# The list of pieces in another order, and GpSimd's subtractions in operations of 512 elements

## The chip, the cores and the metric

The kernel runs on one core of a Trainium2 chip. Its engines work side by side, each through its own instructions in program order: TensorE (PE, with its weight loads as PEld), VectorE (DVE), ScalarE (ACT), GpSimd (POOL) and SyncE (SP), which here issues nearly all transfers. The metric is the time of one execution on the device in microseconds, as the median of several runs.

## The reference

Attention over 32 pooled memory rows per head, and then a two-layer network whose nonlinearity is h - tanh(h):

```python
a = phi - np.max(phi, axis=2, keepdims=True)
a = np.exp(a)
a = a / (np.sum(a, axis=2, keepdims=True) + 1e-09)
k_m = np.einsum('bhsm,bhsd->bhmd', a, k)
v_m = np.einsum('bhsm,bhsd->bhmd', a, v)
scores = scale * np.matmul(q, k_m.transpose(0, 1, 3, 2))
scores = scores - np.max(scores, axis=-1, keepdims=True)
attn = np.exp(scores)
attn = attn / (np.sum(attn, axis=-1, keepdims=True) + 1e-09)
attn_out = np.matmul(attn, v_m)
...
x = attn_out.transpose(0, 2, 1, 3).reshape(B * S, H * D)
h = x @ w_in
g = h - np.tanh(h)
out = g @ w_out
```

There are 8 batches with 8 heads, 576 positions, head width 64 and 32 memory rows; x is 4608 x 512, `w_in` 512 x 2048 and `w_out` 2048 x 512. The weights come as 64-bit floats.

## The kernel before

**Arithmetic.** The pooled values are multiplied into `w_in` first (the pieces P, with result `pp` in PSUM, `ph` and `pl` in SBUF), so that h is a product of the attention weights (256 per token: 8 heads with 32 rows) with P. Every operand of a product is split into a high half in float16 and a low half, the rest after subtracting the high one, and three products of halves stand for one of full precision. ScalarE casts the high half; the low half is a subtraction. The nonlinearity is a polynomial in h times h cubed.

**Tiling.** The 4608 tokens are 18 units (u) of 256, the 2048 features four blocks (fb) of 512. For each unit and block there are: `H` (`mm1`, L598), the product h into the PSUM tile `hs`, and its square on ScalarE (L616); `a` (`cubic`, L621), VectorE (L630), ScalarE (L632) and VectorE again (L642); `g` (L659), the high half; `c` (`a_low`, L664), the low half on GpSimd, or `cv` on VectorE; and `M` (`mm2`), the product with `w_out`. From unit 4 on, `M` uses seven products of half-size blocks instead of eight (L749). For these `f` (`s_forms`, L668) makes four sums of blocks on VectorE (L675), and `s` (`s_high`, L679) their halves, the high ones on ScalarE (L682), the low ones on GpSimd (L684). `BS`, `BF`, `BH` and `BL` make the same sums of `w_out` once. `E` (`evict`, L795) puts the results of a unit together (L800 to L811) and stores them.

**Attention.** For each batch: `FX`, `FA`, `KA`, `KB`, `KR`, `Q`, `QT` load; `X`, `YX`, `XU`, `XT` (batches 0 and 1) or `XP`, `YM`, `YE` make the exponentials, where `YM` calls `less_top` (L208) on GpSimd; `V`, `N`, `U`, `UV` pool and normalise; `S`, `AM`, `AE`, `AD`, `AT`, `AS` are scores and softmax; `P` and `PL` (L578) make P and its low half. `P` takes the one buffer of the PSUM pool `ps_a`, which `S`, `V`, `U`, `XP` and `NI` use too. `T` converts two blocks of a weight from 64-bit words, `L`, `Lv` and `Lp` make their low halves on GpSimd, VectorE or TensorE. `i0:gg` loads block 0 of `w_in` into a buffer named gg, `i6:kv3` blocks 6 and 7 into kv3, `o2` block 2 of `w_out`; `k5:q` loads a block again for a check, which `CW` reads. `Z` (`warm`, L846) is a pair of products whose result is not used.

**Order.** The string `ORDER` (L71 to L130) is the program: its words are taken one after another, each emits one piece, and a word that stands again emits the next step of the same piece (`T0 T0 T0 T0` is three steps on VectorE and the cast on ScalarE). Each engine works through its instructions in that order (`in_order`, L915), SyncE's loads too, and waits only for what an instruction reads or the buffer it writes. There is a second way through the kernel for inputs outside a range (`wide_path`), which doesn't run here.

Of the kernel before, what the change touches and what calls it, by code (L numbers as in the profile page):

```python
# [75 lines left out]
XU1 a0.0 XT1 XU1 T11 T11 a0.0 KA1 o1:gg T11 V1.0 Lv10 g0.0 V1.1 N1 H1.1 H1.0 a1.0 a1.0 o0:pp2 T8 T8 c0.0 U1 UV1 o10:pp5 KA2 UV1 U1 S1.0 T8 H1.1 S1.0  # L76
AM1.0 T8 Lv8 T11 L11 L11 k1:q a1.0 g1.0 FA2 CW1 ap1.1 ap1.1 H0.1 H0.1 i10:kv3 S1.1 S1.1 AM1.1 ap1.1 ap0.1 AM1.0 AE1.0 AD1.0 c1.0 AM1.1 AE1.1 T5 M0.0
M0.0 AD1.0 AD1.1 g1.1 P1.0 P1.0 cv1.1 W0 PL1.0 M1.0 M1.0 ap0.1 AT1.0 AS1.0 AD1.1 AT1.1 ASv1.1 AS1.0 ap0.1 i8:kv2 T4 T5 T5 M1.1 T4 g0.1 cv0.1 FX2 P1.1
P1.1 o8:gg ASv1.1 T5 M1.1 OP1 L5 H2.0 H2.0 o9:pp4 PL1.1 i14:kv3 L5 X2 OP1 a2.0 M0.1 OP0 M0.1 T4 OP0 T12 T12 H2.1 a2.0 a2.0 T12 T4 Lv4 H2.1 a2.1 g2.0
XP2 Y2 a2.1 H3.0 H3.0 M2.0 T12 a2.1 g2.1 o11:gg T13 c2.0 M2.0 H3.1 H3.1 Lv12 ap3.0 ap3.0 P0.2 P0.2 T13 T13 YE2 T13 ap3.0 g3.0 c2.1 M2.1 M2.1 PL0.2  # L80
i12:kv2 V2.0 L13 T7 T7 a3.1 a3.1 KB2 V2.1 N2 T6 T7 T6 T6 H0.2 cv3.0 OP2 OP2 Q2.1 T7 P1.2 H0.2 Q2.0 a3.1 Lv7 FA3 M3.0 M3.0 P1.2 T6 Lv6 g3.1 H1.2 H1.2
PL1.2 a0.2 BS0 a0.2 P0.3 a0.2 P0.3 PL0.3 L13 c3.1 M3.1 M3.1 g0.2 c0.2 ap1.2 ap1.2 U2 U2 o12:kv2 T14 ap1.2 o14:kv3 OP3 OP3 H1.3 T15 W1 UV2 T15 UV2 M0.2
T15 H1.3 a1.3 S2.0 FQ3 S2.0 AM2.0 g1.2 c1.2 H0.3 T15 a1.3 a1.3 g1.3 c1.3 P1.3 P1.3 T14 H2.2 PL1.3 Lv15 H0.3 S2.1 H2.2 a0.3 a2.2 M0.2 a0.3 a2.2 S2.1
AM2.0 AE2.0 a0.3 H2.3 T14 AM2.1 AM2.1 X3 P2.0 P2.0 T14 Lv14 g0.3 H2.3 c0.3 AE2.1 ADv2.1 M1.2 M1.2 M1.3 M1.3 AD2.0 AD2.0 a2.3 a2.2 a2.3 a2.3 g2.2 c2.2
R1 O1 H3.2 H3.2 PL2.0 O1 AT2.0 P2.1 AS2.0 AS2.0 ADv2.1 AT2.1 ASv2.1 P2.1 M0.3 M0.3 ap3.2 ap3.2 H4.0 BF0 g2.3 c2.3 PL2.1 BH0 ap3.2 H4.0 R0 O0 O0 BL0
P2.2 a4.0 P2.2 PL2.2 g3.2 a4.0 BS1 H4.1 QT3.0 P2.3 a4.0 BF1 H3.3 P2.3 f4.0 BH1 PL2.3 cv3.2 M2.2 M2.2 H3.3 H4.1 ASv2.1 g4.0 c4.0 ap3.3 ap3.3 XP3 M2.3
M2.3 Y3 XX BL1 ap3.3 g3.3 a4.1 H4.2 s4.0 s4.0 R2 O2 O2 M3.2 cv3.3 H4.2 a4.2 a4.1 a4.1 f4.1 a4.2 a4.2 f4.2 H4.3 H4.3 g4.1 c4.1 BS2 R3 M3.2 M3.3 M3.3
s4.1 YE3 KR3.0 O3 KR3.1 V3.0 M4.0 M4.0 M4.0 M4.0 a4.3 a4.3 O3 BF2 BH2 g4.2 s4.1 V3.1 M4.1 a4.3 f4.3 QT3.1 BL2 N3 U3 H5.0 UV3 UV3 U3 S3.0 c4.2 BS3 S3.0
AM3.0 s4.2 M4.1 M4.1 M4.1 H5.0 a5.0 s4.2 M4.2 P3.0 BF3 M4.2 a5.0 H5.1 P3.0 a5.0 M4.2 M4.2 f5.0 AM3.0 g4.3 c4.3 k2:q BH3 s4.3 PL3.0 H5.1 a5.1 AE3.0
AD3.0 P3.1 s4.3 s5.0 H5.2 P3.1 PL3.1 BL3 M4.3 a5.1 a5.1 S3.1 S3.1 M4.3 M4.3 M4.3 H5.2 s5.0 W3 AM3.1 g5.0 c5.0 E4 f5.1 M4.3 g5.1 s5.1 AD3.0 P3.2 E4  # L90
a5.2 a5.2 M5.0 E4 E4 E4 H5.3 H5.3 M5.0 AT3.0 c5.1 E4 s5.1 M5.1 k0:e AS3.0 AS3.0 a5.2 g5.2 f5.2 a5.3 CW0 AM3.1 a5.3 FQ4 a5.3 M5.0 AE3.1 c5.2 M5.1 AD3.1
s5.2 H6.0 H6.0 P3.2 k4:q a6.0 a6.0 AD3.1 PL3.2 s5.2 M5.0 M5.1 M5.1 g5.3 a6.0 H6.1 H6.1 f5.3 W2 f6.0 M5.2 M5.2 M5.2 M5.2 s5.3 s5.3 a6.1 g6.0 P3.3 P3.3
H6.2 a6.1 c5.3 c6.0 s6.0 X4 XP4 H6.2 PL3.3 a6.1 CW2 AT3.1 AS3.1 FA4 s6.0 YM4 a6.2 a6.2 KR4.0 f6.1 a6.2 M5.3 M5.3 M5.3 E5 M5.3 M5.3 CW4 H6.3 s6.1 s6.1
E5 M6.0 KR4.1 g6.1 H6.3 a6.3 a6.3 M6.0 E5 AS3.1 H7.0 c6.1 M6.1 E5 E5 E5 YM4 M6.1 M6.0 YE4 V4.0 f6.2 M6.0 M6.1 g6.2 a6.3 f6.3 M6.1 H7.0 a7.0 s6.2 a7.0
s6.3 a7.0 f7.0 H7.1 H7.1 a7.1 g6.3 s6.2 a7.1 V4.1 N4 c6.2 k3:e M6.2 M6.2 g7.0 M6.2 M6.2 a7.1 f7.1 QT4.0 c6.3 SI0 s7.0 s6.3 U4 UV4 H7.2 U4 SS0 H7.2
a7.2 s7.0 M6.3 M6.3 M6.3 E6 M6.3 CW3 FQ5 M6.3 c7.0 E6 S4.0 UV4 a7.2 H7.3 a7.2 f7.2 g7.2 E6 E6 s7.1 s7.1 M7.0 g7.1 S4.0 H7.3 c7.2 k5:e NI0 M7.0 M7.0
M7.0 QT4.1 S4.1 NI0 E6 E6 AM4.0 a7.3 a7.3 H8.0 a7.3 f7.3 g7.3 X5 H8.0 S4.1 c7.1 M7.1 M7.1 M7.1 s7.2 s7.2 a8.0 H8.1 M7.2 M7.2 M7.2 a8.0 a8.0 s7.3 AM4.0
AE4.0 s7.3 c7.3 AM4.1 M7.1 M7.2 H8.1 AD4.0 AD4.0 a8.1 M7.3 M7.3 a8.1 a8.1 f8.0 f8.1 g8.0 M7.3 g8.1 E7 E7 AT4.0 s8.0 AM4.1 s8.0 P4.0 P4.0 PL4.0 H8.2
H8.2 a8.2 AE4.1 AD4.1 E7 E7 a8.2 a8.2 M7.3 M7.3 E7 f8.2 P4.1 P4.1 E7 H8.3 H8.3 a8.3 FA5 CW5 c8.0 M8.0 M8.0 M8.0 M8.0 c8.1 AS4.0 AS4.0 H9.0 s8.1 s8.1
KR5.0 M8.1 g8.2 c8.2 a8.3 a8.3 PL4.1 XP5 M8.1 M8.1 s8.2 M8.1 H9.0 KR5.1 g8.3 a9.0 H9.1 a9.0 f8.3 s8.3 a9.0 f9.0 YM5 H9.1 s8.2 P4.2 P4.2 PL4.2 YM5 M8.2  # L100
M8.2 QT5.0 M8.2 YE5 M8.2 c8.3 V5.0 g9.0 AD4.1 a9.1 a9.1 a9.1 g9.1 f9.1 s8.3 H9.2 H9.2 s9.0 M8.3 M8.3 M8.3 AT4.1 k6:e V5.1 M8.3 M8.3 E8 E8 c9.0 s9.0 N5
E8 SI1 a9.2 E8 E8 s9.1 P4.3 P4.3 PL4.3 c9.1 E8 a9.2 M9.0 a9.2 f9.2 M9.0 g9.2 M9.0 U5 SS1 U5 UV5 FQ6 s9.2 UV5 H9.3 s9.1 M9.1 NI1 H9.3 NI1 a9.3 AS4.1
M9.0 CW6 S5.0 S5.0 QT5.1 s9.2 a9.3 M9.1 a9.3 f9.3 AS4.1 H10.0 AM5.0 M9.1 g9.3 M9.1 k7:q H10.0 a10.0 AM5.0 AE5.0 AD5.0 CW7 S5.1 c9.2 S5.1 a10.0 H10.1
a10.0 f10.0 M9.2 H10.1 a10.1 s9.3 c9.3 P5.0 M9.2 M9.2 M9.2 P5.0 PL5.0 AM5.1 a10.1 a10.1 X6 s9.3 s10.0 s10.0 H10.2 H10.2 a10.2 AD5.0 M9.3 W5 M9.3 f10.1
a10.2 a10.2 g10.0 c10.0 M9.3 M9.3 AT5.0 s10.1 M9.3 XP6 YM6 H10.3 P5.1 H10.3 M10.0 E9 E9 M10.0 E9 M10.0 k8:e CW8 P5.1 AM5.1 AE5.1 s10.1 E9 E9 E9 M10.0
AS5.0 g10.2 AS5.0 g10.1 W4 c10.1 a10.3 H11.0 FA6 f10.2 s10.2 M10.1 M10.1 a10.3 a10.3 P5.2 KR6.0 M10.1 M10.1 H11.0 PL5.1 a11.0 a11.0 a11.0 P5.2 PL5.2
H11.1 c10.2 YM6 YE6 g10.3 V6.0 s10.2 M10.2 M10.2 M10.2 H11.1 QT6.0 KR6.1 M10.2 f10.3 s10.3 s10.3 f11.0 s11.0 a11.1 a11.1 AD5.1 AD5.1 AT5.1 H11.2 AS5.1
# [284 lines left out]
def split_path(ctx, tc, c, ins, out):  # L392
# [271 lines left out]
    def a_low(u, fb, eng):  # L664
        for x, (hi, lo) in a_parts(u, fb):
            eng.tensor_tensor(lo, x, hi, op=ALU.subtract)  # L666
# [463 lines left out]
```

## Time and profile before

| | |
|---|---|
| three runs, us | 671.54, 672.4, 670.91 |
| median, us | 671.54 |
| the profiled execution: its own time, us | 672.69 |
| its span from first to last instruction, us | 670.9 |
| mean granted TensorE clock | 0.984 |
| ScalarE busy, us | 402.4 |
| moved by DMA | 85.03 MB, mean 127 GB/s |

The span is 1.8 us shorter than the time of the execution it was taken from. In the profile an engine's busy time is the sum of its instructions' spans without overlap. Rows of a group give the line, engine, operation, tiles out<-in, sizes and count, then total busy us and mean ns, then the engine's idle time just before these instructions and what ended it. Rows of the timeline give start and duration in us. "x2" in a row of the timeline merges two instructions that follow each other. The granted clock is 1.00 at full speed.

### The profile page before, as it was taken

How to read it: one execution, taken by the hardware profiler on the slowest of the kernel's cores; microseconds unless marked ns; L12 is line 12 of the kernel's file. 1: busy time of each engine (PE TensorE's matmuls, PEld its weight loads, DVE VectorE, ACT ScalarE, POOL GpSimd, SP SyncE). 2: the span in 40 equal slices, each digit the busy share in tenths (PEclk: the TensorE clock that was granted, in tenths of full speed). 3: DMA queues.
4: the chain of work that ended last, by engine and by line, in shares of the span. 5: the costliest groups of instructions: out<-in, count | busy, mean ns of one | idle time of the engine just before them, and what ended most of it. 6: DMA issues, size and time to landing. Idle time of an engine off the chain costs nothing. (4 is left out here: it accounts for less than half of the span.)

```text
span 670.9 us, 16165 instructions
## 1 busy us (share of the span) xinstructions
PE 633.5 (94%) x6882; PEld 485.1 (72%) x6882; DVE 584.8 (87%) x818; ACT 402.4 (60%) x541; POOL 371.5 (55%) x257
## 2 busy tenths in 40 slices
...
GB/s 330 310 355 216 195 190 205 149 97 64 34 198 107 67 34 68 146 169 127 2 69 114 163 99 37 150 94 130 36 147 164 162 75 88 30 127 69 122 95 38
DMA packets 25872, 85.03 MB, mean 127 GB/s; under 512 B 2752, under 2 KB 2752, under 8 KB 25024
## 3 DMA queue, kind: packets, MB, share of 16 engines
...
## 5 line engine op out<-in xcount | busy, mean ns | idle before, releaser
L666 POOL TENSOR_TENSOR g<-h,g 128x256 f16<-128x256 f32 (+1 forms) x123 | 149.0, 1232 | 111.0 <-ACT g L662 106.6
L609 PEld LDWEIGHTS <-ph 128*128 128x128 f16 x2304 | 177.5, 98 | 28.0 <-issue 12.0
L684 POOL TENSOR_TENSOR f<-s,f 128x1024 f16<-128x1024 f32 x56 | 125.7, 2245 | 84.1 <-ACT f L682 65.6
L609 PE MATMUL hs<-ah,ph 128*128 128x256 f16 (+3 forms) x1152 | 151.5, 246 | 2.1 <-DVE h L630 2.0
L761 PEld LDWEIGHTS <-f 128*128 128x128 f16 x1344 | 128.8, 98 | 31.4 <-issue 12.1
L761 PE MATMUL x<-bt,f 128*128 128x256 f16 x1008 | 128.4, 273 | 4.4 <-DVE r L802 2.0
L609 PE MATMUL hs<-al,ph 128*128 128x256 f16 (+3 forms) x576 | 127.6, 246 | 0.2 <-POOL al L551 0.2
L632 ACT ACTIVATE u<-u,beta 128x1024 f32<-128x1024 f32 x72 | 82.6, 1147 | 61.7 <-DVE h L630 60.7
L642 DVE SCALAR_TENSOR_TENSOR h<-u,h 128x1024 f32<-128x1024 f32 x72 | 98.5, 1369 | 19.8 <-ACT u L632 19.5
L761 PEld LDWEIGHTS <-g 128*128 128x128 f16 x1008 | 98.6, 98 | 13.7 <-issue 1.1
L616 ACT ACTIVATE u<-hs 128x1024 f32<-128x1024 f32 x54 | 55.1, 1020 | 52.9 <-PE hs L609 31.2
L662 ACT ACTIVATE g<-h 128x512 f16<-128x512 f32 (+2 forms) x128 | 68.4, 580 | 23.6 <-DVE h L642 19.7
L630 DVE SCALAR_TENSOR_TENSOR h<-hs,u 128x1024 f32<-128x1024 f32 x54 | 65.6, 1214 | 13.8 <-ACT u L616 9.9
L682 ACT ACTIVATE f<-s 128x1024 f16<-128x1024 f32 x56 | 58.8, 1050 | 25.5 <-DVE s L675 19.8
L742 PEld LDWEIGHTS <-g 128*128 128x128 f16 x384 | 36.7, 98 | 48.1 <-issue 3.9
L675 DVE TENSOR_TENSOR s<-h 128x256 f32<-128x256 f32 x112 | 59.5, 571 | 1.8
L742 PE MATMUL o<-wout_hi,g 128*128 128x512 f16 x192 | 59.0, 379 | 2.2 <-ACT g L662 2.2
L609 PE MATMUL h<-ah,ph 128*128 128x256 f16 (+3 forms) x384 | 51.1, 248 | 0.0
L761 PE MATMUL o<-wout_hi,f 128*128 128x256 f16 x224 | 46.5, 275 | 1.2 <-DVE r L811 1.2
L761 PE MATMUL o<-wout_hi,g 128*128 128x256 f16 x224 | 46.5, 275 | 0.0
L761 PE MATMUL x<-wout_hi,g 128*128 128x256 f16 x224 | 45.9, 273 | 0.5 <-POOL g L666 0.5
L761 PE MATMUL o<-bt,g 128*128 128x256 f16 x336 | 45.9, 274 | 0.0
...
## 6 DMA issues: line engine op xcount, KB each, us to landing
...
```

Of the source, the lines that this page charges most:

```text
L609: nc.tensor.matmul(hp[:, k, tu : tu + w], px[:, g, cs], d[ax][:, g, ta : ta + w], start=(n == 0), stop=(n == 5),)
L616: nc.scalar.activation(uu, hp, AF.Square, scale=1.0 / (S_A * S_P))
L630: nc.vector.scalar_tensor_tensor(h3, hp, C2 * S_G / (S_A * S_P), uu, op0=ALU.mult, op1=ALU.mult)
L632: nc.scalar.activation(uu, uu, AF.Square, bias=c["beta"])
L642: nc.vector.scalar_tensor_tensor(h3, uu, CC, hp, op0=ALU.add, op1=ALU.mult)
L662: nc.scalar.activation(hi, x, AF.Copy)
L666: eng.tensor_tensor(lo, x, hi, op=ALU.subtract)
L675: nc.vector.tensor_tensor(o, x, y, op=op)
L682: nc.scalar.activation(f[:, 0], s, AF.Copy)
L684: nc.gpsimd.tensor_tensor(f[:, 1], s, f[:, 0], op=ALU.subtract)
L742: nc.tensor.matmul(o, gx[:, k, P * tt : P * tt + P], wx[:, 4 * fb + k, :], start=(first and k == 0 and wx is wout_hi and gx is gh), stop=( ...
L761: nc.tensor.matmul(dst, a(na, kk), b(nb, kk), start=(new and kk == 0 and na == 0 and nb == 0), stop=(end and kk == 1 and na == 1))
```

## The change

Two things change. The words of `ORDER` stand in another order from the first to the last; both lists have 1707 words, and every word is in both equally often. Four functions cut what they give to GpSimd into operations of 512 elements per partition: `less_top` (there for batches 4 to 7 on GpSimd, VectorE's calls stay whole), `a_low` for the units below 4 (the later ones have 512 and 256 already), `s_high` and `b_low`. The elements computed are the same.

```diff
 ORDER = """
-i3:pp5 i1:gg i0:gg T0 T0 FX0 Z0.0 Z0.0 Z0.0 Z0.0 X0 T0 i6:kv3 T3 T3 T3 i4:kv2 Z0.0 Z0.0 Z0.0 Z0.0 Z0.0 Z0.0 Z0.0 Z0.0 Z0.0 Z0.0 Z0.0 T2 T2 Z0.0 T2
-Z0.0 Z0.0 Z0.0 Z0.0 i2:gg T1 T1 Z0.0 KA0 Z0.0 Z0.0 Z0.0 Z0.0 Z0.0 YX0 XU0 T0 Lp0 T3 Lp3 XT0 Lp0 T1 KB0 XT0 T2 o2:gg V0.0 XU0 V0.1 o3:gg Lp3 Lv2 Q0.0
-N0 T9 U0 U0 S0.0 Q0.1 T1 T9 L1 T9 o4:gg L1 S0.0 S0.1 AM0.0 AM0.0 UV0 o6:gg UV0 o5:pp2 S0.1 AM0.1 T9 AM0.1 AE0.0 AD0.0 AE0.1 Lp9 Q1.0 AD0.1 o7:gg P0.0
-P0.0 AD0.0 PLp0.0 PLp0.0 AT0.0 ASv0.0 T10 P0.1 P0.1 KB1 AD0.1 AT0.1 Lp9 ASv0.0 AS0.1 AS0.1 T10 T10 T10 H0.0 H0.0 PL0.1 H1.0 FX1 Q1.1 X1 a0.0 YX1 XT1
...
+i0:gg Z0.0 i1:gg i6:kv3 T0 T0 T0 T0 Z0.0 Z0.0 T3 T3 T3 T3 FX0 Z0.0 Z0.0 Z0.0 i2:gg Z0.0 Z0.0 Z0.0 Z0.0 Z0.0 i3:pp5 Z0.0 X0 YX0 Z0.0 Z0.0 Z0.0 Z0.0 Lp0
+Lp0 i4:kv2 T1 T1 T1 Z0.0 T1 KA0 KB0 Z0.0 Lp3 L1 L1 T2 Z0.0 XU0 Z0.0 XT0 XT0 V0.0 T2 T2 o2:gg Z0.0 Z0.0 Lp3 T2 Lv2 XU0 V0.1 N0 U0 UV0 Z0.0 Z0.0 Z0.0
+o3:gg T9 T9 Q0.0 T9 Q0.1 U0 S0.0 S0.0 AM0.0 AM0.0 S0.1 S0.1 UV0 AM0.1 T9 Lp9 AE0.0 AM0.1 AE0.1 AD0.0 AD0.0 P0.0 P0.0 AD0.1 AT0.0 ASv0.0 Z0.0 AD0.1
+o4:gg o5:pp2 Lp9 PLp0.0 PLp0.0 o7:gg P0.1 T10 P0.1 AT0.1 AS0.1 KA1 ASv0.0 o6:gg T11 FX1 T10 T10 T10 PL0.1 X1 H0.0 AS0.1 H1.0 H0.0 KB1 a0.0 YX1 XT1
...
 def less_top(self, eng, e, m):
-        eng.tensor_tensor(
-            e[:, 0:8].rearrange("p (c r) x -> p c (r x)", r=2), e[:, 0:8].rearrange("p (c r) x -> p c (r x)", r=2),
-            m.unsqueeze(1).to_broadcast((P, 4, 256)), op=ALU.subtract,
-        )
+        for i in range(0, 8, 8 if eng is self.tc.nc.vector else 4):
+            n = 4 if eng is self.tc.nc.vector else 2
+            x = e[:, i : i + 2 * n].rearrange("p (c r) x -> p c (r x)", r=2)
+            eng.tensor_tensor(x, x, m.unsqueeze(1).to_broadcast((P, n, 256)), op=ALU.subtract)
...
     def a_low(u, fb, eng):
         for x, (hi, lo) in a_parts(u, fb):
-            eng.tensor_tensor(lo, x, hi, op=ALU.subtract)
+            for i in (0, 2) if x.shape[1] == 4 and eng is nc.gpsimd else (None,):
+                ks = slice(None) if i is None else slice(i, i + 2)
+                eng.tensor_tensor(lo[:, ks], x[:, ks], hi[:, ks], op=ALU.subtract)
...
-        nc.gpsimd.tensor_tensor(f[:, 1], s, f[:, 0], op=ALU.subtract)
+        for i in (0, 2):
+            nc.gpsimd.tensor_tensor(f[:, 1, i : i + 2], s[:, i : i + 2], f[:, 0, i : i + 2], op=ALU.subtract)
...
     def b_low(fb):
-        for k in range(0, 4, 2):
-            ks = slice(k, k + 2)
-            nc.gpsimd.tensor_tensor(bts[fb][:, 1, ks], bts["w", fb][:, ks], bts[fb][:, 0, ks], op=ALU.subtract)
+        for k in range(4):
+            nc.gpsimd.tensor_tensor(bts[fb][:, 1, k], bts["w", fb][:, k], bts[fb][:, 0, k], op=ALU.subtract)
```

More of the change, by code (lines that the diff above doesn't have):

```diff
@@ L76 @@
[L76 to L107, printed above, removed]
@@ L124 @@
-a15.3 c15.1 H16.0 g15.2 c15.2 M15.1 M15.1 k25:q CW25 M15.1 M15.1 k14:q k31:q s15.2 H16.0 k30:q a16.0 a16.0 H16.1 a16.0 SO3 g16.0 g15.3 c15.3 k20:q
-f15.3 s15.3 s15.3 M15.2 SS3 M15.2 M15.2 M15.2 c16.0 NO3 CW14 H16.1 a16.1 a16.1 H16.2 CW31 M15.3 H16.2 a16.1 g16.1 c16.1 M15.3 CW30 M15.3 M15.3 M15.3
-f16.0 CW20 s16.0 s16.0 a16.2 a16.2 E15 E15 E15 E15 f16.1 NO3 H16.3 a16.2 E15 M16.0 E15 M16.0 M16.0 s16.1 H16.3 M16.0 a16.3 a16.3 k29:q g16.2 s16.1
-M16.1 c16.2 f16.2 H17.0 s16.2 s16.2 a16.3 CW29 H17.0 g16.3 c16.3 M16.1 M16.1 a17.0 a17.0 a17.0 f16.3 s16.3 f17.0 M16.1 M16.2 H17.1 NO3 H17.1 s16.3
@@ new lines @@
+H1.1 o9:pp4 a1.0 ap1.1 Q1.1 S1.1 FA2 c0.0 M0.0 S1.0 AM1.0 H0.1 ap0.1 S1.1 AM1.0 T11 L11 ap1.1 ap1.1 AE1.0 P1.0 g1.0 L11 AD1.0 P1.0 PL1.0 c1.0 M1.0
+AM1.1 AD1.0 M1.0 ap0.1 ap0.1 P1.1 g1.1 cv1.1 KB2 AM1.1 AE1.1 AD1.1 P1.1 AT1.0 i10:kv3 PL1.1 AD1.1 AS1.0 AS1.0 AT1.1 ASv1.1 T5 M1.1 M1.1 ASv1.1 T5 H2.0
+g0.1 cv0.1 OP1 i8:kv2 OP1 T5 H2.0 T4 T5 L5 T4 T4 FX2 a2.0 a2.0 L5 X2 T4 o8:gg M0.1 OP0 M0.1 T12 T12 H2.1 H2.1 i14:kv3 a2.0 g2.0 i12:kv2 Lv4 OP0 XP2
+c2.0 Y2 H3.0 H3.0 YE2 KA2 a2.1 a2.1 T12 o11:gg T13 a2.1 Q2.1 T12 M2.0 M2.0 Lv12 g2.1 P0.2 P0.2 ap3.0 PL0.2 H3.1 H3.1 T13 ap3.0 T13 T6 T13 L13 V2.0
@@ new lines @@
+V2.1 c2.1 N2 T6 ap3.0 g3.0 a3.1 a3.1 T6 T6 M2.1 OP2 P1.2 M2.1 T7 T7 P1.2 OP2 L13 o14:kv3 Q2.0 H1.2 H1.2 Lv6 cv3.0 H0.2 T7 T7 a3.1 ap1.2 PL1.2 g3.1
+c3.1 H0.2 a0.2 Lv7 a0.2 a0.2 T15 T15 M3.0 M3.0 M3.1 ap1.2 ap1.2 o12:kv2 g0.2 P0.3 P0.3 FQ3 OP3 PL0.3 M3.1 U2 UV2 T15 U2 UV2 OP3 H1.3 H1.3 T14 BS0 T14
+g1.2 S2.0 S2.0 AM2.0 H0.3 P1.3 M0.2 c0.2 a1.3 H0.3 a1.3 c1.2 a0.3 a0.3 a1.3 T14 T15 k1:q Lv15 a0.3 AM2.0 P1.3 PL1.3 AE2.0 M0.2 g1.3 H2.2 c1.3 H2.2
+AD2.0 a2.2 S2.1 AD2.0 AT2.0 g0.3 H2.3 S2.1 AM2.1 a2.2 H2.3 a2.3 c0.3 T14 Lv14 BF0 M1.2 AS2.0 a2.2 a2.3 P2.0 FA3 a2.3 P2.0 BH0 H3.2 H3.2 g2.2 CW1 R1
```

67 lines of the change are left out of this document (48 added, 19 removed).

## The prediction

> **What bounds the kernel now.** I read the page's busy times first, then the same by stage, then what TensorE waits for.
>
> ```profile
> span 670.9 us, 16165 instructions
> PE 633.5 (94%) x6882; PEld 485.1 (72%) x6882; DVE 584.8 (87%) x818; ACT 402.4 (60%) x541; POOL 371.5 (55%) x257
> ```
>
> TensorE (PE) is idle for 670.9 - 633.5 = 37.4 us. VectorE (DVE) follows at 87%; GpSimd (POOL) is busy for little more than half. Both lists hold the same 1707 pieces, each as often, so TensorE's work cannot change: only its 37.4 us of idle time and the time at a lowered clock can. The stages show where these lie (columns: stage, length, then busy us of PE, PEld, DVE, ACT, POOL, granted clock, DMA share, GB/s):
>
> ```profile
> 0.00:43.00 43.00, 34.20 (x268) 14.79 (x268) 28.20 (x49) 16.77 (x21) 7.67 (x15) 0.82 0.84 323
> 43.00:60.00 17.00, 13.25 (x172) 10.48 (x164) 15.77 (x27) 12.07 (x17) 3.55 (x2) 0.95 0.73 277
> 180.00:262.00 82.00, 77.09 (x815) 56.53 (x814) 75.21 (x96) 46.56 (x60) 53.45 (x32) 1.00 0.29 97
> 400.00:460.00 60.00, 54.35 (x684) 45.42 (x683) 47.02 (x68) 33.38 (x55) 37.26 (x27) 0.97 0.26 91
> 560.00:660.00 100.00, 96.15 (x1029) 85.14 (x1014) 85.15 (x126) 61.20 (x86) 61.84 (x44) 1.00 0.24 80
> 660.00:670.90 10.90, 5.33 (x48) 4.49 (x48) 3.45 (x13) 0.66 (x2) 0.00 (x0) 0.93 0.17 57
> ```
>
> The idle time is 8.8 us up to 43 us (the first attention), 3.8 up to 60, then 4.9, 5.7 and 3.9 in three later stages, and 5.6 in the tail. That is 32.6 of the 37.4; the stages left out share 4.8 and are as good as full. In the tail, the last sum waits for the last product in either list, so I leave it. There are 37.4 - 8.8 - 5.6 = 23.0 us between 43 and 660 that an order and a less hindered VectorE could change.
>
> What TensorE waits for, the longest first (total, times, longest):
>
> ```profile
> PE pp L560 <- DVE ph L578: 6.0, 3, 2.6
> ...
> PE hs L609 <- DVE h L630: 2.0, 4, 0.9
> PE x L761 <- DVE r L802: 2.0, 2, 1.0
> ...
> PE pkv L274 <- DMA kv<-in_kva_dram: 1.4, 2, 0.9
> ...
> PE x L761 <- POOL f L684: 0.7, 1, 0.7
> ```
>
> It waits for VectorE 10.0 us in three of these rows, for a load 1.4 and for the forms of GpSimd 0.7 us, once. So a later GpSimd hurts little, and an earlier VectorE is what helps.
>
> **Part 1: operations of 512 elements on GpSimd.** What VectorE loses to GpSimd shows where a long GpSimd operation runs:
>
> ```profile
> 515.13 4.60 POOL L684 TENSOR_TENSOR f<-s,f 128x1024 f16<-128x1024 f32 x2
> 519.70 2.77 POOL L666 TENSOR_TENSOR g<-h,g 128x512 f16<-128x512 f32 x2
> ```
> ```profile
> 515.38 2.35 DVE L806 TENSOR_TENSOR r<-r 128x256 f32<-128x256 f32 x1
> ...
> 520.08 1.85 DVE L642 SCALAR_TENSOR_TENSOR h<-u,h 128x1024 f32<-128x1024 f32 x1
> ```
>
> L806 adds 256 elements and takes 2.35 us: it ends at 517.73, shortly after the first of the two `f` operations must have ended (515.13 + 2.13, the time of one alone by a row below). The second `f` has its full time after that: 4.60 is 2.13 + 0.34 + 2.13. So VectorE gets in between two GpSimd operations that follow each other. L642 shows it again inside a pair of 512 and 256.
>
> The same groups over the whole run, first with their means, then each line's shortest, median and longest in ns:
>
> ```profile
> L642 DVE SCALAR_TENSOR_TENSOR h<-u,h 128x1024 f32<-128x1024 f32 x72 | 98.5, 1369 | 19.8 <-ACT u L632 19.5
> ...
> L675 DVE TENSOR_TENSOR s<-h 128x256 f32<-128x256 f32 x112 | 59.5, 571 | 1.8
> ...
> L675 DVE TENSOR_TENSOR s<-h,s 128x256 f32<-128x256 f32 x56 | 32.8, 585 | 1.9
> ```
> ```profile
> L642 DVE SCALAR_TENSOR_TENSOR h<-u,h x72: 1182/1219/2594, 51.0 to 650.1; 128x1024 f32<-128x1024 f32 x72
> ```
> ```profile
> L675 DVE TENSOR_TENSOR s<-h x112: 382/418/2587, 182.0 to 651.8; 128x256 f32<-128x256 f32 x112
> L675 DVE TENSOR_TENSOR s<-s,h x56: 410/418/1373, 182.6 to 654.0; 128x256 f32<-128x256 f32 x56
> L675 DVE TENSOR_TENSOR s<-h,s x56: 424/425/2357, 183.1 to 655.4; 128x256 f32<-128x256 f32 x56
> ```
>
> The median stands next to the shortest, so it is the undisturbed time, and the mean above it is what some of them waited. The excess is 72 x 0.150 + 112 x 0.153 + 56 x 0.160 = 10.8 + 17.1 + 9.0 = 37 us of VectorE's 584.8, spent behind GpSimd.
>
> ```profile
> 323.03 2.13 POOL L684 TENSOR_TENSOR f<-s,f 128x1024 f16<-128x1024 f32 x1 [3.87 <-issue]
> ```
> ```profile
> L666 POOL TENSOR_TENSOR g<-h,g x2: 662/908/1153, 329.3 to 330.4; 128x512 f16<-128x512 f32 x1, 128x256 f16<-128x256 f32 x1
> ```
>
> An operation of 1024 takes 2.13 us alone, one of 512 takes 1.15, so two of 512 cost 0.17 us more. The change splits 79 operations: 56 forms, 11 low halves of the first four units (the other five are on VectorE), 8 of the block sums and 4 of `less_top`. **GpSimd gains** 79 x 0.17 = 13 us of work, plus what VectorE does in between. I cost this at nothing: GpSimd is idle for 670.9 - 371.5 = 299 us, and TensorE waited for its forms 0.7 us in the row above. If that cover were gone in one product of four, 14 x 0.17 is 2.4 us.
>
> **VectorE wins** this: the operations that are split are 79 x 2.13 = 168 us of GpSimd's 371.5. A wait behind one lasts on average half of it, 1.07 us, and 0.58 afterwards, 46% less. By their share of GpSimd's time 45% of the 37 us stand behind them; as the longer operations also make the longer waits, it may be two thirds. 46% of that is 8 to 11 us, and I take 10. It has to come through the 23.0 us of gaps on TensorE, of which those behind VectorE are the larger part; elsewhere TensorE sets the pace and takes nothing from a faster VectorE. I take 3 us. The bounds are 0 (none of the gaps stands behind a hindered VectorE operation) and 10 (all that the three rows of waits name).
>
> **Part 2: the order from the first product on.** No row shows the new order. Counting the listed pieces with the durations of the rows, I find the first `H` of unit 8 behind the same TensorE work as before, within 1 us, and of unit 16 within 0.2 us; at no unit does VectorE's listed work before `H` move by more than 5.5 us. I also counted, for each `H`, whether the VectorE work listed up to the freeing of its PSUM bank is longer than the TensorE work listed meanwhile. It is so 18 times in the old list and 20 times in the new, 29.4 and 29.5 us in sum. The loads on SyncE's queue move with the list too: every `i`, `o`, `k`, `KR`, `Q` stands behind other loads than before, and each waits for the buffer that it takes. TensorE waited 1.4 us for loads of `kv`, and I cost their move within the same bounds. I take 0, with 4 us to both sides: the 5.7 us that the stage from 400 to 460 lost, and no other like it, is the size of one bad place.
>
> **Part 3: the start.** The list issues blocks i0 and i1 first, where i3 stood ahead of them; T0 needs only those two. The filling products `Z` are as many, 26, but 10 of them now stand behind the first `Lp0`, between the products of the first attention; all 26 stood ahead.
>
> ```profile
> 24.00:28.00 4.00, 2.87 (x50) 1.85 (x50) 2.77 (x8) 1.09 (x2) 0.00 (x0) 0.54 0.87 353
> 28.00:32.00 4.00, 2.35 (x33) 0.68 (x32) 3.96 (x7) 3.49 (x5) 1.39 (x1) 0.50 0.22 67
> 426.00:430.00 4.00, 3.55 (x37) 2.22 (x38) 2.70 (x3) 2.64 (x4) 2.24 (x2) 0.64 0.41 149
> ```
> ```profile
> 15.90 1.02 PE L472 MATMUL pw<-wt,idw 128*128 128x512 f32 x2
> ```
> ```profile
> 43.35 0.40 PE L609 MATMUL h<-ah,ph 128*128 128x256 f16 x1
> ```
> ```profile
> L851 PE MATMUL warm<-nid 128*128 128x512 f16 x52 | 14.1, 443 | 1.7 <-DVE nid L1079 1.7
> ```
> ```profile
> 32.38 2.07 PE L472 MATMUL pw<-wt,idw 128*128 128x512 f32 x2 [1.66 <-DVE vl L534]
> ```
>
> Half a megabyte less ahead of T0 is 0.52 MB / 323 GB/s = 1.6 us for the first conversion. But X0 and its exponentials now stand behind T3 on VectorE, the score branch starts no earlier, and the conversion that precedes the first scores has the same 16.8 us of listed VectorE work ahead of it. I give 1 us of the 1.6 to the end of the stage. The clock was 0.50 to 0.54 from 24 to 32 us, and at 32 the same product pair took 2.07 us instead of 1.02. On the path to the first `H`, at 43.35, lie `Lp9` (four such halves, 2.3 us lost) and the first `P` (about 1). The 10 fillers put TensorE to work there, and can also stand in the way; I take 1 of those 3.3 us. Sum of the start: -2, between -4.9 (all of both) and +1 (two fillers of 0.54 us in front of the scores).
>
> [...]
>
> **Sum.** -2 (start) - 3 (less waiting behind GpSimd) + 0 (order) + 0 (GpSimd's own 13 us) = -5. The profiled execution took 672.69 us by its own time, 1.8 more than its span, and would be 667.7. It lies 1.15 above the median of 671.54, so the predicted median is **666.5 us**.
>
> **The rivals.**
> - *The clock stays up in the start.* If the ten fillers hold it, all 3.3 us come, and the sum is -1.6 - 3.3 - 3: 663.6. For it: they stand exactly where the clock was low. Against: the 0.54 came while TensorE was 72% busy, and ten fillers, 14.1 / 26 = 0.54 us each, add 5.4 us over some 20.
> - *VectorE's relief reaches nobody.* The splits don't shorten waits because VectorE finds the second half as busy as the first: only the start is left, 669.5. Against: L806 got in between.
> - *Nothing.* The start and the order cancel: 671.5. For it: the counted lists are alike.
> - *A new gap, slower.* The `P` of an attention uses one PSUM bank that `PL` on VectorE must empty; where it comes late TensorE stops, and its clock falls:
>
> ```profile
> 426.45 0.41 PE L560 MATMUL pp<-win_hi,vh 64*32 64x512 f16 x8 [2.55 <-DVE ph L578]
> ```
>
>   The price is the 2.55 us of the gap and 4 x 0.36 of lost clock in the window from 426 to 430, 4.0 us. Two more such places than the old list has, with the other gains halved, give 671.5 + 8 - 2.5 = 677; it decides from the second one on. For it: every piece has a new place. Against: there were two such gaps in 32 pieces.
>
> **How the numbers follow.** The forecast has 0.42, the clock 0.13, no relief 0.08, nothing 0.14, the new gap 0.23. A difference of 0.2% (1.3 us) is about what a measurement of this kernel can tell from none. The first three are faster by more: 0.63; same 0.14; slower 0.23. The range reaches down to 660.5, the clock's case with 3 of the 4 us by which an order may be better, and up to 675.0, into the new gap's case; it leaves out about half of that case, 0.12, and 0.05 below.
>
> **What would show it.** The mean of L675 `s<-h` falls from 571 ns towards 530 and that of L642 from 1369 towards 1330: part 1 is right. The granted clock between 24 and 32 us above 0.54 and the first `H` ahead of 43.35: the start is right. TensorE's busy time stays near 633 and its idle time falls to about 32. It is wrong if GpSimd's pieces of 512 take much more than 1.15 us, if a wait of a product for `f` grows beyond 3 us in all, or if waits of `pp` for L578 exceed 6.0 us.

## The result, and the profile after

The changed kernel takes **643.81 us** (643.38 to 644.82, 4 runs), the kernel before on the same chip 671.22 (667.36 to 672.4, 4 runs). The ratio is 0.9603 with an interval of 0.9563 to 0.9644: 27 us faster, where 5 were forecast, and below the whole range. The head of its page, and the same stages as before (stage, length, busy us of PE, PEld, DVE, ACT, POOL, granted clock, DMA share, GB/s):

```profile
span 642.7 us, 16248 instructions
PE 622.9 (97%) x6882; PEld 482.5 (75%) x6882; DVE 573.1 (89%) x818; ACT 402.2 (63%) x541; POOL 378.9 (59%) x336
```
```profile
0.00:43.00 43.00, 34.39 (x300) 16.35 (x301) 33.60 (x57) 21.00 (x27) 9.71 (x16) 0.96 0.89 341
43.00:60.00 17.00, 15.50 (x204) 11.24 (x204) 16.43 (x25) 12.98 (x22) 2.71 (x3) 1.00 0.89 347
180.00:262.00 82.00, 79.95 (x928) 62.88 (x926) 74.46 (x99) 48.01 (x66) 55.12 (x46) 1.00 0.26 88
400.00:460.00 60.00, 60.00 (x771) 51.22 (x768) 50.75 (x80) 37.86 (x55) 42.99 (x39) 1.00 0.36 119
460.00:560.00 100.00, 100.00 (x1289) 85.82 (x1286) 87.90 (x135) 70.51 (x102) 69.69 (x62) 1.00 0.23 77
560.00:632.00 72.00, 72.00 (x678) 64.47 (x677) 65.52 (x97) 43.40 (x57) 47.62 (x43) 1.00 0.35 118
```

From 400 us on TensorE is without a gap to the tail, and its idle time is 642.7 - 622.9 = 19.8 us, 17.6 less than before. Its busy time fell by 10.6 us as well, with as many matmuls (6882): so what the page calls busy is not work alone. Time at a lowered clock counts in it (in the trace before, the pair of products of L472 takes 1.02 us at 15.90 and 2.07 at 32.38, where the clock was 0.50; mean clock 0.984 before, 0.996 now), and perhaps small waits inside groups of matmuls; how much each makes isn't shown. What TensorE still waits for between 60 and 660 us, the longest first (total, times, longest):

```profile
PE o L745 <- DVE pr L841: 1.7, 1, 1.7
PE pkv L275 <- DVE ph L579: 1.4, 1, 1.4
PE hs L610 <- DVE h L631: 0.9, 2, 0.6
PE pp L561 <- DVE ph L579: 0.3, 1, 0.3
```

The 6.0 us of `pp` for the low half of P are 0.3. VectorE's groups and GpSimd's forms (lines moved by 1 to 4):

```profile
L643 DVE SCALAR_TENSOR_TENSOR h<-u,h 128x1024 f32<-128x1024 f32 x72 | 95.8, 1332 | 7.2 <-ACT u L633 6.9
...
L678 DVE TENSOR_TENSOR s<-h 128x256 f32<-128x256 f32 x112 | 51.2, 497 | 1.3
...
L367 DVE TENSOR_SCALAR sz<-sz 128x18 f32<-128x18 f32 x16 | 6.8, 426 | 0.5
```
```profile
L688 POOL TENSOR_TENSOR f<-s,f 128x512 f16<-128x512 f32 x112 | 139.9, 1269 | 93.0 <-ACT f L685 75.6 <-issue 7.2 <-DVE sz L367 3.8
```
```profile
L688 POOL TENSOR_TENSOR f<-s,f x112: 1144/1160/2179, 182.6 to 631.4; 128x512 f16<-128x512 f32 x112
```

The means fell as far as part 1 wanted (1332; 497, even below 530). But the second of them didn't fall by the cut, as the next section shows.

### The profile page after: what moved, and what is told of

Same layout as the page of the kernel before. It is cut to its first block, busy times and chain, and to the rows that moved or that the text cites. A ratio compares the mean times of both kernels' runs of the same rounds, so it can differ in the third digit from the quotient of the medians.

```text
span 642.7 us, 16248 instructions
## 1 busy us (share of the span) xinstructions
PE 622.9 (97%) x6882; PEld 482.5 (75%) x6882; DVE 573.1 (89%) x818; ACT 402.2 (63%) x541; POOL 378.9 (59%) x336
## 4 chain that ended last, share of the span: by engine, by line
PE 69%; DVE 21%; ACT 4%; issue 2%; DMA 2%; POOL 1%; DVEq 0%; ACTq 0%; POOLq 0%; SPq 0%
PE x L764 20%; PE hs L610 20%; PE o L764 15%; PE o L745 3%; DVE h L643 3%; DVE h L631 3%; PE pp L561 2%; DVE s L678 2%; DMA raw<-in_w_out_dram 2%; PE o1h L745 2%; DVE ph L579 2%; PE warm L854 2%; PE pkv L275 2%; DVE wt L445 1%; DVE bw L704 1%
## 5 line engine op out<-in xcount | busy, mean ns | idle before, releaser
L688 POOL TENSOR_TENSOR f<-s,f 128x512 f16<-128x512 f32 x112 | 139.9, 1269 | 93.0 <-ACT f L685 75.6
L669 POOL TENSOR_TENSOR g<-h,g 128x512 f16<-128x512 f32 (+1 forms) x134 | 142.5, 1085 | 84.8 <-ACT g L663 74.3
L643 DVE SCALAR_TENSOR_TENSOR h<-u,h 128x1024 f32<-128x1024 f32 x72 | 95.8, 1332 | 7.2 <-ACT u L633 6.9
L678 DVE TENSOR_TENSOR s<-h 128x256 f32<-128x256 f32 x112 | 51.2, 497 | 1.3
```

Of the source, the lines that this page charges most:

```text
L643: nc.vector.scalar_tensor_tensor(h3, uu, CC, hp, op0=ALU.add, op1=ALU.mult)
L669: eng.tensor_tensor(lo[:, ks], x[:, ks], hi[:, ks], op=ALU.subtract)
L678: nc.vector.tensor_tensor(o, x, y, op=op)
L688: nc.gpsimd.tensor_tensor(f[:, 1, i : i + 2], s[:, i : i + 2], f[:, 0, i : i + 2], op=ALU.subtract)
```

## Which of the two, the list or the cut

Four kernels: one part of the change without the other, and, with all operations cut, each list's words up to its first `H` followed by the other list's remaining words.

```diff
 # new list, operations as before
 # old list, operations cut
 # cut; new list to the first H, then the old list's remaining words
 # cut; old list to the first H, then the new list's remaining words
```

> The new list with GpSimd's operations uncut. Theory A (the order removes the gaps; the cut operations are a few us): 645 to 651 us. Theory B (VectorE's shorter waits behind GpSimd close the gaps, and a gap on TensorE is worth more than its own length): 657 to 667 us, the order alone gives the 4.2 us by which the first H is earlier and a little more. The mean of the VectorE row s<-h is near 571 ns again in both.

> The old list with GpSimd's operations cut to 512 elements. Theory A: 666 to 671 us, little changed. Theory B: 650 to 659 us. First H at 43 us as before in both. The sum of both parts' gains should be 27 us if they add up; if it is less than 20, order and cut need each other.

> Cut operations; the new list up to the first H, then the words that are left in the old list's order. If the start's lead lasts to the end: 4 us less than the old list with cut operations. If the gaps that follow swallow it: within 1.5 us of that.

> Cut operations; the old list up to the first H, then the words that are left in the new list's order. If the start's lead lasts to the end: 643.8 + 4 = 648 us. If it is swallowed: 644 to 645. Under theory A this one is close to the changed kernel, and the one with the new head close to the old.

| kernel | median us | ratio to before, interval |
|---|---|---|
| new list, not cut | 662.2 | 0.9895 (0.9838 to 0.9952) |
| old list, cut | 670.96 | 1.0011 (0.9981 to 1.0041) |
| new start, old rest, cut | 666.73 | 0.9952 (0.9921 to 0.9982) |
| old start, new rest, cut | 648.81 | 0.9689 (0.9634 to 0.9745) |

The cut alone gives nothing, the list alone about 8.7 us (670.9 in that comparison), both together 27. The parts don't add up: **cutting is worth 0 in the old list and 662.2 - 643.81 = 18.4 us in the new one.** The start gives 670.96 - 666.73 = 4.2 or 648.81 - 643.81 = 5.0 us, the list behind it 670.96 - 648.81 = 22, both with cut operations. (The kernel before took 670.9 to 672.2 us in the median beside the experiments, so a difference between medians of two groups of experiments is good to about 1 us.)

The page's head for the new list with nothing cut parts the two gains:

```profile
span 659.9 us, 16168 instructions
PE 624.0 (95%) x6882; PEld 481.5 (73%) x6882; DVE 590.7 (90%) x818; ACT 402.6 (61%) x541; POOL 361.0 (55%) x257
```

In these executions the list alone took TensorE's busy time from 633.5 to 624.0 us (its mean clock is 1.00 in this execution) and left its idle time at 659.9 - 624.0 = 35.9 us, against 37.4. The cut in the new list left the busy time (622.9) and took the idle time to 19.8.

VectorE's means, new list with nothing cut, then old list cut:

```profile
L676 DVE TENSOR_TENSOR s<-h 128x256 f32<-128x256 f32 x112 | 49.9, 486 | 1.3
```
```profile
L642 DVE SCALAR_TENSOR_TENSOR h<-u,h 128x1024 f32<-128x1024 f32 x72 | 100.5, 1396 | 19.9 <-ACT u L632 19.7
...
L677 DVE TENSOR_TENSOR s<-h 128x256 f32<-128x256 f32 x112 | 58.6, 563 | 2.8 <-POOL f L687 1.1
```

So the fall of `s<-h` from 571 to 497 ns is the list's (486 with nothing cut), and in the old list the cut leaves both means about where they were (563 and 1396, against 571 and 1369).

## Which operations

In the new list: the forms alone cut; all but the forms cut; the second half of a form ahead of the first; and forms in four pieces.

```diff
 # forms only: a_low, less_top and b_low as before
 # all but forms
-        for i in (0, 2):
-            nc.gpsimd.tensor_tensor(f[:, 1, i : i + 2], s[:, i : i + 2], f[:, 0, i : i + 2], op=ALU.subtract)
+        nc.gpsimd.tensor_tensor(f[:, 1], s, f[:, 0], op=ALU.subtract)
 # halves turned
-        for i in (0, 2):
+        for i in (2, 0):
 # quarters
+        for i in range(4):
+            nc.gpsimd.tensor_tensor(f[:, 1, i], s[:, i], f[:, 0, i], op=ALU.subtract)
```

> The new list; only the low halves of the 56 forms are cut, the other 23 operations are whole. If the cut forms carry the difference between 662.2 (nothing cut) and 643.8 (all cut), it is spread over the units as they are, so 56 of 79: 644 to 649 us. If the other 23 carry it: 657 to 662.

> The new list; all cut but the forms. The mirror of the run before: 657 to 662 us if the forms carry the difference, 644 to 649 if the other 23 do. The two runs' gains over 662.2 should add up to 18.4 if the cuts act one by one.

> The changed kernel, with the second half of each form first. The first product of M reads the first half, which now comes 1.15 us later, as late as in a whole operation; VectorE's waits stay as short. Theory C (VectorE waits less): 643 to 646 us. Theory D (the first product finds its half earlier): 655 to 662 us, with waits of x for f on TensorE of 3 us or more.

> The changed kernel with the forms in four operations of 256 elements. GpSimd's work grows by another 112 x 0.17 = 19 us. Theory C: VectorE's busy time falls by another 3 to 8 us, and as TensorE is full the time by 0 to 4: 640 to 644 us. Theory D: 643 to 645. If GpSimd becomes late: 646 or more, with waits of x for f.

Forms only: 647.5 us, ratio 0.9645 (0.9609 to 0.9682). All but forms: 658.19, 0.9795 (0.9765 to 0.9825). By the medians the forms are worth 14.7 of the 18.4 us and the other 23 operations 4.0; by the ratios to the kernel before, 16.8 and 6.7 of 19.6. The forms carry most of it either way. Halves turned: 647.33, 0.9637 (0.9607 to 0.9667). Quarters: 647.06, 0.9631 (0.9601 to 0.9661).

What the forms hold up is seen in the new list with nothing cut. These are TensorE's waits there, for its products and then for its weight loads:

```profile
PE hs L610 <- DVE h L631: 3.7, 5, 1.5
PE x L762 <- POOL f L685: 2.5, 4, 1.7
```
```profile
PEld L762 <- POOL f L685: 4.1, 5, 1.9
```

In the new list products and their weights wait for `f` at 2.5 and 4.1 us; in the old list these were 0.7 and 1.4. With the cut both rows for `f` are gone, but for 0.2 us of a weight load. Turned halves bring them back though VectorE's busy time is 573.0 as in the changed kernel:

```profile
PEld L764 <- POOL f L688: 4.2, 6, 1.3
...
PE x L764 <- POOL f L688: 2.7, 4, 1.0
```

So a part of the gain, some 3.5 us by the medians (2.3 by the ratios, whose intervals overlap, so the waits say it more surely than the time), is that the first product finds the first half a whole operation earlier. The rest goes with VectorE: its busy time is 590.7 with nothing cut and 573.1 with all, and TensorE's waits for it between 60 and 660 us, all rows added, fall from 12.5 to 4.3 us. Turned halves keep both gains (573.0 and 3.2 us). In the old list the cut takes only 5.0 us off VectorE's 584.8, and the same sum stays: 12.8 before, 13.6 after it. The 17.6 us of busy time don't come from the additions `s<-h` (49.9 us uncut, 51.2 cut); its largest parts are 6.1 us of the small `sz` operations in the last section, 3.7 of the additions `r<-r,r` and 3.0 of `s<-h,s`.

Quarters are no better than halves, as GpSimd's and VectorE's rows show:

```profile
L688 POOL TENSOR_TENSOR f<-s,f 128x256 f16<-128x256 f32 x224 | 164.4, 764 | 76.7 <-ACT f L685 66.6 <-issue 6.7 <-ACT stat L505 3.2
```
```profile
L678 DVE TENSOR_TENSOR s<-h 128x256 f32<-128x256 f32 x112 | 58.8, 565 | 1.3
```

Quarters were expected to give up to 4 us, or to show waits for `f`; they did neither. Four pieces take 3.06 us where two took 2.54, and the additions, at 486 ns with whole forms and 497 with halves, are at 565. That a VectorE operation meets a piece more often is a guess that would fit. The traces show where a VectorE operation gets long: of the 112 `s<-h`, all that take over 600 ns, 22 in the kernel before and 12 in the changed one, overlap a GpSimd operation and end within 0.6 us after it; of the shorter ones 10 and 21 overlap one. The longest takes 2587 ns with whole forms in the old list and 1490 with halves in the new one, where the median is 418 in both. That shorter instructions need not mean less waiting in sum is what 565 ns adds.

## Where the list gains: two places

The old list's trace (here with cut operations) shows two long stops of VectorE, both near unit 10:

```profile
408.74 0.77 DVE L374 STREAM_TRANSPOSE af<-sc 128x576 f32<-128x576 f32 x1
413.67 0.42 DVE L802 SCALAR_TENSOR_TENSOR r<-x,r 128x256 f32<-128x256 f32 x1 [4.16 <-ACT ph L573]
...
423.18 1.58 DVE L642 SCALAR_TENSOR_TENSOR h<-u,h 128x1024 f32<-128x1024 f32 x1 [2.22 <-ACT u L632]
```
```profile
421.05 1.06 ACT L684 ACTIVATE f<-s 128x1024 f16<-128x1024 f32 x1 [4.29 <-DVE s L677]
422.01 1.14 ACT L632 ACTIVATE u<-u,beta 128x1024 f32<-128x1024 f32 x1
```
```profile
413.30 0.27 PE L763 MATMUL x<-wout_hi,g 128*128 128x256 f16 x1
414.60 1.47 PE L763 MATMUL x<-bt,f 128*128 128x256 f16 x12 [1.03 <-DVE r L804]
```

L802 is the first step of `E(9)`, and the list has it behind the first piece of `M(10)`, which writes the other half of the same PSUM tile `x`. The profile names a cast on ScalarE as what it waited for, but it starts 0.10 us after that piece ends on TensorE (413.30 + 0.27 = 413.57), so I take it to have waited for the piece. The next piece of `M(10)` waits in turn for L804, 1.03 us. In the second place the cast `s10.2` stands on ScalarE ahead of the square that `a10.3` needs, and waits itself for VectorE's additions. The new list has neither. Two kernels mend both places in the old list (and the second step of `E(10)`), cut and not cut; one puts the two arrangements into the new list.

```diff
 # old list
-M10.0 E9 E9 M10.0 E9 M10.0
+E9 E9 M10.0 M10.0 E9 M10.0
-a10.3 H11.0 FA6 f10.2 s10.2 M10.1 M10.1 a10.3 a10.3
+a10.3 H11.0 FA6 f10.2 M10.1 M10.1 a10.3 s10.2 a10.3
-M11.0 E10
+E10 M11.0
 # new list: all six E9 moved behind the first M10.0
+AS5.0 M10.0 E9 E9 M10.0 E9 a10.2 M10.0 M10.0 E9 E9 E9
-a10.3 a10.3 P5.2 g10.2 f10.2 s10.2 a10.3
+a10.3 f10.2 s10.2 a10.3 P5.2 g10.2 a10.3
```

> The old list with cut operations, and three words of it moved: the first two steps of E(9) and the second of E(10) ahead of the first M of the next unit, and the cast s10.2 behind ScalarE's step of a10.3. Theory 'places' (the old list loses its time in a few places where VectorE, and ScalarE ahead of it, stand at the head of their queue for a step listed too early or behind the wrong one): VectorE's idle 4.2 us before E(9) and 2.2 us before the last step of a10.3 go, E(10) starts 4 to 6 us earlier than in the old list with cut operations, and the time falls from 670.96 to 665 to 667. Theory 'spread' (the new order's 22 us come from many small moves, and a stall taken away here is met again at the next one): E(10) at most 2 us earlier and the time within 2 us of 670.96.

> The kernel before with the same three words moved and nothing cut. Theory 'VectorE's pace' (cutting pays only where VectorE sets the pace; every stall of VectorE for something else that is taken away makes the cut worth more): slower than the run with cut operations and the same words by more than the 0.3 us that separate the two kernels with the unchanged old list, by 1 to 3 us: 667 to 669. Rival (the worth of the cut has to do with this list's places as little as before): the same as the run with cut operations to within 0.7 us.

> The changed kernel with the old list's two arrangements put into its list at the same places: E(9) behind the first M of unit 10, and f10.2 and s10.2 between VectorE's first and ScalarE's step of a10.3. Theory 'places': the 4 and 2 us come back on VectorE there, the time rises by 3 to 6 us, to 647 to 650. Theory 'spread': the later work has room to take them up, 643.8 to 645.

Mended and cut: 667.91 us, 0.9952 (0.9921 to 0.9982). Mended, not cut: 666.01, 0.9936 (0.9904 to 0.9967). New list with both: 650.96, 0.9707 (0.9664 to 0.975). The start of the first step of `E(u)` on VectorE in each trace places the difference:

| list | E(8) | E(9) | E(10) | E(17) |
|---|---|---|---|---|
| old, cut | 373.91 | 413.67 | 448.17 | 661.26 |
| old, cut, mended | 374.68 | 410.21 | 444.92 | 658.48 |
| changed kernel | 362.96 | 395.02 | 427.99 | 635.17 |
| changed, both put in | 363.13 | 399.44 | 436.04 | 643.53 |

In the mended list `E(9)` starts without a wait:

```profile
410.21 0.38 DVE L802 SCALAR_TENSOR_TENSOR r<-x,r 128x256 f32<-128x256 f32 x1
```

From E(8) to E(9) it gains 39.76 - 35.53 = 4.2 us, and keeps 3.6 of them to the end (it was 0.77 behind at E(8) and is 2.78 ahead at E(17)). The second place gives nothing there: 34.50 us from E(9) to E(10) become 34.71. In the new list the first arrangement costs 36.31 - 32.06 = 4.2 us, with the wait back in front of the same step:

```profile
399.44 0.42 DVE L803 SCALAR_TENSOR_TENSOR r<-x,r 128x256 f32<-128x256 f32 x1 [4.20 <-ACT ph L574]
```

The stretch up to E(10), with the second one and what the first still displaces, costs 36.60 - 32.97 = 3.6. From there to E(17) nothing is taken up or added (207.49 and 207.18). So "places" holds for **7 of the 22 us** as measured in the new list (in the old one, both cut, 3 by the medians and 4 by the ratios, less than the expected 4 to 6), and these two stalls, put into a full list, are paid in full.

The starts of `E` say roughly where the 22 us arise. The old start with the new list is ahead of the old list, both cut, by 5.5 us at E(4) (235.84 against 241.37), 7.4 at E(8), 15.1 at E(9), 14.9 at E(12), 20.2 at E(14) and 22.4 at E(17). So some 5 us lie ahead of E(4) and some 5 between E(12) and E(14), where no experiment was made.

The other expectation fell: cutting is worth nothing more once the two stops are gone (667.91 cut, 666.01 not, with intervals that overlap). That these stops hide the cut's worth in the old list is not so; what does is open.

## The start: fillers and loads

Three kernels: the new list with its ten later `Z` ahead of the first `Lp0`; the old list, cut, with ten of its `Z` behind the first `Lp0`; the changed kernel with three `Z` more.

```diff
 # new list: ten Z0.0 taken out behind Lp0
+Z0.0 Z0.0 Z0.0 Z0.0 Z0.0 Z0.0 Z0.0 Z0.0 Z0.0 Z0.0 Lp0
 # old list, cut: the last ten Z0.0 taken out ahead of Lp0
+Lp0 Z0.0 Z0.0 T3 Lp3
+Z0.0 Z0.0 V0.0 XU0 V0.1 o3:gg Lp3 Z0.0 Z0.0 Lv2 Q0.0 N0 Z0.0 Z0.0 Z0.0
+AT0.0 Z0.0 ASv0.0
 # changed kernel, three Z more
+S0.0 S0.0 Z0.0 AM0.0
+T9 Z0.0 Z0.0 Lp9
```

> The changed kernel with its ten filling products of the start moved back ahead of the first product Lp0, as in the old list. Theory 'the fillers hold the clock': the granted clock from 24 to 36 us falls from 1.00, 0.81, 0.77 towards 0.54 and 0.50, the first H comes 1 to 3 us later than 39.15, and the time is 645 to 647. Rival 'the loads do it' (T0 starts 2.2 to 3.5 us earlier because blocks i0 and i1 are loaded first, and the rest of the start follows): the first H within 0.5 us of 39.15 or earlier, and the time 643 to 644.5.

> The old list with cut operations, and ten of its 26 filling products moved behind the first product Lp0, between the products of the first attention; the loads stay as they were. Theory 'fillers': TensorE's idle places there are covered, the granted clock from 24 to 36 us rises from 0.50 and 0.54 to 0.75 or more, the first H comes 2 to 5 us earlier than 43.35, and the time falls from 670.96 to 666 to 669. Rival 'fillers and loads belong together' (in the new list the loads of i0 and i1 first make the room in which the fillers stand; here VectorE comes to the first attention's steps no earlier, so TensorE only warms up for nothing): the first H at 42.8 to 43.5 and the time 670 to 671.5, whatever the clock shows.

> The changed kernel with three filling products more: one behind the second S0.0 and two ahead of the first Lp9, where TensorE is idle for 0.97 and 1.29 us and the clock is 0.77 to 0.81. Theory 'fillers': the clock from 28 to 36 us rises above 0.9, the four halves of Lp9 (1.54 and 1.91 us a pair) come down towards 1.02 a pair, and the first H comes 0.5 to 1.5 us ahead of 39.15: 642.3 to 643.5. Rival: three times 0.54 us of work on TensorE's path take back what the clock gives, 643.6 to 645.

The stages from 24 to 36 us, first the changed kernel, then the one with its fillers first:

```profile
24.00:28.00 4.00, 2.52 (x32) 1.11 (x40) 3.97 (x10) 0.78 (x3) 0.00 (x0) 1.00 1.00 397
28.00:32.00 4.00, 2.71 (x20) 1.12 (x13) 3.47 (x7) 1.50 (x3) 2.31 (x2) 0.81 1.01 371
32.00:36.00 4.00, 3.39 (x37) 0.72 (x43) 3.64 (x9) 1.78 (x3) 2.31 (x2) 0.77 0.64 251
```
```profile
24.00:28.00 4.00, 3.33 (x60) 2.64 (x64) 1.23 (x1) 2.31 (x4) 1.94 (x1) 0.50 1.01 402
28.00:32.00 4.00, 2.45 (x46) 1.01 (x46) 2.61 (x9) 0.45 (x2) 0.00 (x0) 0.50 0.07 27
32.00:36.00 4.00, 2.02 (x33) 0.77 (x18) 3.97 (x8) 1.06 (x1) 1.16 (x1) 0.50 0.57 201
```
```profile
23.96 1.95 PE L275 MATMUL pkv<-kv,e 128*32 128x129 f32 x32 [2.96 <-ACT e L251]
```
```profile
39.15 0.28 PE L610 MATMUL h<-ah,ph 128*128 128x256 f16 x1
```
```profile
45.75 0.28 PE L610 MATMUL h<-ah,ph 128*128 128x256 f16 x1
```

Fillers first: 649.91 us, 0.9688 (0.9646 to 0.9731), **6.1 us slower** by where ten pairs of products without a use stand, more than either expectation allowed. In its trace (of an execution of 651.47 us) TensorE is idle for 2.96 us ahead of the first attention, the clock is 0.50 for the next 12 us, and the first `H` comes at 45.75 instead of 39.15. The first conversion is as early in it as in the changed kernel, whose row is the first here (before it began at 8.51):

```profile
5.05 0.43 DVE L439 TENSOR_SCALAR wt<-raw 128x512 uint32<-128x512 uint32 x1 [3.22 <-DMA raw<-in_w_in_dram]
```
```profile
5.23 0.43 DVE L439 TENSOR_SCALAR wt<-raw 128x512 uint32<-128x512 uint32 x1 [3.39 <-DMA raw<-in_w_in_dram]
```

So the earlier loads do nothing by themselves: with them and the fillers first, the time is 649.91, and 648.81 with the whole old start. With the fillers alone moved, in the old start, the clock is 0.98 to 1.00 from 24 to 36 us and the first `H` comes at 39.32, but the time is 669.33, 0.9981 (0.9953 to 1.0009), only 1.6 us below the same kernel with its fillers ahead, where `H` came at 40.33. The interval reaches past 1, so it allows for no change, and the time lies between the two expectations. By the medians the fillers need the new list's loads, or something else in its start, for the whole 4 to 5 us; the intervals don't settle it.

One trace is a thin basis for the clock. The words up to the first `H` are the same in several of these kernels, and their traces differ:

| start | trace | mean clock of the execution | clock, 28 to 32 us | 32 to 36 us | first H, us |
|---|---|---|---|---|---|
| old | kernel before | 0.984 | 0.50 | 0.50 | 43.35 |
| old | old list, cut | 0.988 | 0.58 | 0.57 | 40.33 |
| old | old start, new rest, cut | 0.992 | | | 40.54 |
| new | changed kernel | 0.996 | 0.81 | 0.77 | 39.15 |
| new | new start, old rest, cut | 0.996 | | | 38.99 |
| new | new list, not cut | 1.00 | | | 38.02 |

From 28 to 36 us the clock in the changed kernel's trace is above that in both traces of the old start. The mean clock of a whole execution, which holds the other stages too, is 0.992 to 1.00 in 40 executions of kernels with the new start's words, and 0.98 to 0.994 in 104 with the old start's. But the new start's first `H` is only 1.2 to 2.5 us earlier than in the two other traces of the old start; the trace of the kernel before is of an execution in which it came late. The rest of the 4 to 5 us comes later: with the new list behind both starts, the new one leads by 1.4 us at the first `H` (39.15 against 40.54) and by 3.5 at E(4) (232.30 against 235.84).

Three more fillers change nothing: 644.39, 0.9608 (0.9582 to 0.9633). In that trace the clock is 1.00 from 24 to 36 us, the two `Lp9` pairs take 1.13 and 1.02 instead of 1.54 and 1.91 us, and `H` comes at 38.62. The new list with nothing cut has a mean clock of 1.00 over its whole execution and its first `H` at 38.02 without them, so that the three did it isn't shown. From 36 to 44 us the clock is then 0.79 instead of 1.00.

The 2.96 us of idle TensorE in the kernel with its fillers first stand ahead of a clock of 0.50. Shorter gaps stand beside either clock. In the kernel before, gaps of 1.12 and 0.68 us stand beside a clock of 0.54 from 24 to 28 us; in the old list with cut operations, whose start is the same, gaps of 1.11 and 0.67 us stand beside 1.00, and the fall comes later:

```profile
24.00:28.00 4.00, 1.47 (x34) 0.50 (x29) 3.69 (x11) 2.17 (x3) 0.00 (x0) 1.00 0.85 345
28.00:32.00 4.00, 2.93 (x18) 0.84 (x19) 3.54 (x6) 1.74 (x4) 3.67 (x3) 0.58 0.75 264
```

So the length of a gap alone doesn't decide.

## Why the prediction was wrong

- **The step that failed** is the sum: "-2 (start) - 3 (less waiting behind GpSimd) + 0 (order) + 0 (GpSimd's own 13 us)" takes the list and the cut as separate terms, each sized on the old list's trace. Alone they measured -8.7 (the start in it) and 0; the other 18 us are there only together. The term of the cut, "I take 3 us" with bounds 0 and 10, was 0 in the old list and 18.4 in the new one, beyond its bound. That bound was the wait for VectorE in three rows of the old trace (12.8 us between 60 and 660 us with all rows). Part 1 also gave an earlier half of a form no worth, because "TensorE waited for its forms 0.7 us". That held for the old list. In the new one uncut forms hold up products and weight loads, 2.5 and 4.1 us, and TensorE's waits for VectorE shrink with the cut, which they don't in the old list.
- **Part 2**, "I take 0, with 4 us to both sides": without the cut the list is worth 8.7 less the start's 4 to 5, at the edge of that bound; with it, 22. The counts behind the 0 added up the work listed ahead of each `H`. They can't see a step that stands behind a piece that it doesn't need, nor a cast that holds the next square up on ScalarE, and these two arrangements alone cost 7 us in the new list. "The size of one bad place", 5.7 us of idle TensorE in that stage, comes out at 4.2 us of time in either list for the place ahead of E(9).
- **Part 1's mechanism** held in part: a piece of 512 takes 1.16 us in the median, as forecast, and VectorE waits less behind such pieces (the longest `s<-h` takes 1490 ns, where it took 2587). But the relief depends on the list: 10 us of busy time were forecast from the old list, where it was 5.0, and in the new list it was 17.6. And the sign named for it came true by luck. The mean of `s<-h` fell below 530 by the list alone (486 ns with nothing cut); by the cut alone it is 563, and that of L642 rose to 1396.
- **The start** was -2 and measured -4.2 to -5.0. "I take 1 of those 3.3 us" for the fillers is the undersized term: without their places the new start is 6.1 us slower, and 1 us for the earlier loads is not there by itself. The rival in which the clock stays up was nearer: from 28 to 36 us it is 0.77 to 0.81 in the changed kernel, where the old start has 0.50 to 0.58. But the first `H` at 43.35 and the 0.54, which the prediction went by, belong to one execution of the old start, with an `H` that two other traces don't show so late (40.33 and 40.54), and much of the gain shows only behind the first `H`.
- "TensorE's busy time stays near 633" was wrong (622.9), and so was "its idle time falls to about 32" (19.8). Busy time holds time at a lowered clock too (2.07 us for a pair of products that takes 1.02 at 1.00), so the 23.0 us of gaps were no upper bound.
- The **new gap** didn't come: `pp` waits 0.3 us where over 6.0 was to show it.

Open: some 15 of the list's 22 us lie in no place that was tried, and why the cut gives nothing in the old list is only described, so the cause of the 18 us that need both is not shown beyond the waits above. Small gaps stand along the whole old list; of the cut one, the stretches up to E(5), E(6) and E(15), with 1.5, 1.3 and 1.0 us without TensorE:

```profile
241.00:277.00 36.00, 34.46 (x419) 29.92 (x418) 32.79 (x47) 25.03 (x43) 24.93 (x22) 1.00 0.30 93
277.00:308.00 31.00, 29.69 (x341) 25.75 (x339) 26.12 (x37) 17.71 (x24) 22.18 (x20) 1.00 0.41 133
...
581.00:611.00 30.00, 29.04 (x294) 26.08 (x292) 24.79 (x39) 18.28 (x25) 18.98 (x18) 1.00 0.31 106
```
